# A three-stage kernel (attention, two MoE products): instructions freed from the written order from the last group of the first MoE on

## The chip, the cores and the metric

The kernel runs on one core of a Trainium2 chip. The metric is the device time of one execution in microseconds (us); less is better. A core has five engines that matter here: TensorE (PE, matmuls), VectorE (DVE), ScalarE (ACT), GpSimd (POOL) and SyncE (SP). SP computes nothing here: it issues the loads and stores, which 16 DMA engines carry out. Each engine takes the instructions of its own list in order, and an instruction that waits holds up those behind it.

## What is computed

The reference is an attention, then a product with a cosine gate, then a product with a rational gate. It comes down to:

```python
x = attention(rmsnorm(q) * g_q, rmsnorm(k) * g_k, v)   # 4 batches, 12 heads, 448 rows, 64 columns
x = x.transpose(0, 2, 1, 3).reshape(1792, 768)
h = x @ moe_w_in                                       # 768 x 2048
x = (h * cos(h)) @ moe_w_out                           # 2048 x 768
h = x @ moe2_w_in
P = a[0] + a[1] * h + a[2] * h**2 + a[3] * h**3
Q = 1.0 + abs(b[0]) * abs(h) + abs(b[1]) * h**2
out = (P / (Q + 1e-6)) @ moe2_w_out
```

## The kernel before

**Weights and numbers.** Every fp32 operand of a big product is kept as a high and a low half, and three matmuls take the place of one. A block of 128 columns of `w_in` is a tile "in f", a block of 128 rows of `w_out` a tile "out f", f from 0 to 15; either holds 768 KB with both halves. They are made once and stored in DRAM (`wd`), and loaded again with `load_w` whenever they are used. In this text "in f" and "out f" are tiles of the second MoE. They live in seven places (pool `w`), and from the second MoE on in nine (`w4` adds two).

**The first MoE** goes batch by batch, with the attention of the next batch in between. Its 16 blocks f are taken in four groups of four (`G`). In the last group of the last batch (`tail` in `run`) the six result tiles y are finished; each is split by ACT (high half) and by POOL or DVE (low half) into a tile x and stored to DRAM (`xd<-x`, the line with `self.xd[b, d]` in `moe1_second`).

**The second MoE** (`moe2`) makes two passes, over batches 0 and 1 and over batches 2 and 3. Its work comes in steps:

- A first product (`before`): 18 matmuls of in f with the x of one batch, into one of three PSUM places (`h3_ps`). Then comes the gate (`act2`): ACT makes q, v and w from the PSUM, DVE makes two products with it, which frees the PSUM, then ACT and DVE go on to the two halves of the tile g.
- A second product (`after`): 24 matmuls of four tiles out f with 128 rows of four tiles g, into one of two PSUM places (`o_ps`). ACT copies the first result of a row tile to o, DVE adds the other three to it, and after the fourth it is stored (`out<-o`). A pass has seven row tiles t.

First products of one group and second products of the group before alternate on PE. A group ends with its seventh second product; then the first product with the next group's first tile in f stands in the list. The four tiles out f of one group, the four tiles in f of the next and what is loaded ahead share the nine places: a tile's load overwrites a place whose old tile has been read for the last time.

**What sets the order.** Two things. First, `Clock`, a planner in the kernel: each step is given to it with a duration, and it hands the steps out in the order in which they would be ready. This order, in which the program's text is executed, is the written order. Second, the builder, which makes one list for each engine out of all instructions, with its own costs, and gives each tile one of its pool's places. It may reorder what doesn't depend on each other. The class `InOrder` stops it: each engine's handle (`self.nc.tensor` and so on, made in `Engines`) wraps every call and ties the new instruction to the last one of that engine (`add_manual_dep`, no semaphore). So before, every engine's list is the written order from the first instruction to the last. All instructions go through this helper, which is why the profile puts nearly all of them down to L193; tiles tell them apart.

Of the kernel before, what the change touches and what calls it, by code (L numbers as in the profile page):

```python
# [36 lines left out]
class Clock:  # L37
# [5 lines left out]
    def __init__(self):  # L43
        self.t, self.n, self.named = 0.0, 0, {}
        self.free = dict.fromkeys(("V", "A", "G", "S"), 0.0)
        self.todo = {e: [] for e in self.free}
        self.tab, self.dma = None, 0.0
# [133 lines left out]
class InOrder:  # L181


    def __init__(self, tc, engine):
        self.tc, self.engine, self.last = tc, engine, None

    def __getattr__(self, name):
        fn = getattr(self.engine, name)
        if not callable(fn):
            return fn  # L190

        def call(*args, **kw):
            inst = fn(*args, **kw)  # L193
            if hasattr(inst, "ins"):
                if self.last is not None:
                    info = mybir.DependencyInfo(
                        mybir.DependencyClass.NoSync, mybir.DependencyReason.DATA
                    )
                    self.tc.add_manual_dep(inst.ins, self.last.ins.name, info)
                self.last = inst  # L200
            return inst

        return call


class Engines:
# [4 lines left out]

    def __getattr__(self, name):
        return getattr(self.core, name)


class Kernel:
# [741 lines left out]
    def run(self):  # L958
        tc, nc, ck = self.tc, self.nc, self.ck
# [25 lines left out]
        def places(n, p, shape, dt, name):  # L985
            return Ring(n, lambda: p.tile(shape, dt, tag=name, name=name))
# [59 lines left out]
        def s_visits(ns):  # L1046

            it = s_chunks(ns)
            for k in ((1, 2, 3, 2, 2) if len(ns) == 2 else ()):
                fns = [next(it) for _ in range(k)]  # L1050
                yield lambda: [fn() for fn in fns]
            assert next(it, None) is None

        def v_visits(ns):

            a = [(n, kb) for n in ns for kb in range(NC)]
            for i in range(0, len(a) + 2, 2):
                yield lambda i=i: (
                    [self.att_va(st[n], kb) for n, kb in a[max(i - 2, 0) : i]],
                    [self.att_vt(st[n], kb) for n, kb in a[i : i + 2]],  # L1060
                )

        def take(it, k):
            for _ in range(k):
                fn = next(it, None)
                if fn is None:
                    return
                fn()
# [5 lines left out]
        def ring(name, n, shape, side="left"):  # L1074
            p = self.pool(name, n, side, PS)
            return p, Ring(n, lambda: p.tile(shape, F32, tag="t", name=name))
# [36 lines left out]
        def predecode(every):  # L1113
            steps[0] += 1
            flying[:] = [k for k in flying if k.end is None or k.end > ck.t]
            if ahead and steps[0] % every == 0 and len(flying) < 3:
                flying.append(self.decode(*ahead.popleft(), False, 4))

        m2 = None
        for b in range(B):  # L1120
            if b == B - 1:
                ck.emitted(*(("x", b, j) for j in range(NJ)), *chain.from_iterable(self.h_ring.used))
                self.close(x_ps, at_ps, self.at_p)
                self.close(h_ps)
                h_ps, self.h_ring = ring("h3_ps", 3, [P, 512])
                o_ps, self.o_ring = ring("o_ps", 2, [P, 2, 512], "right")
                nl2_p = self.pool("nl2", 1, "right")
                self.g2_ps, self.g2_n = [self.pool("g2", 5, "right")], 0
                yo_p = self.pool("yo", 2, "right")
                self.yo_ring = places(2, yo_p, [P, 2, S], F32R, "x")  # L1130
            vs = empty
            for g in range(NG):
                fs = list(range(g * G, g * G + G))
                gs = dict(head)
                head = {}
                if b == B - 1 and g == 1:
                    self.load_x(0, p=3)
                for f in fs:
                    if f not in gs:
                        gs[f] = self.moe1_first(b, f, lambda: take(vs, 1))  # L1140
                        if b:
                            predecode(2 if b < B - 1 else 1)
                for fn in vs:
                    fn()
                if g + 1 < NG:
                    head = {fs[-1] + 1: self.moe1_first(b, fs[-1] + 1)}
                elif b + 1 < B:
                    head = {0: self.moe1_first(b + 1, 0)}
                ss = vs = empty
                if b + 1 < B and g < 3:  # L1150
                    ns = [(b + 1) * NJ + 2 * g + i for i in range(2)]
                    ss = s_visits(ns)
                    vs = v_visits(ns)
                if g == 0:
                    if b:
                        ck.emitted(*(("xd", b - 1, d) for d in range(KD)))
                    y = self.y_p.tile([P, KD, S], F32, tag="y", name="y")
                tail = b == B - 1 and g == NG - 1
                if tail:
                    while ahead:  # L1160
                        self.decode(*ahead.popleft(), False, 4)
                    self.load_x(1)
                    self.nl_p, nl1_p = nl2_p, self.nl_p
                    m2 = self.moe2([0, 1], G, [2, 3])
                    lead, nxt = next(m2)
                for d in range(KD):
                    take(ss, 1)
                    self.moe1_second(b, d, fs, gs, y)
                    if b:
                        predecode(2 if b < B - 1 else 1)  # L1170
                    if tail and d % 2:
                        next(lead)
                for fn in ss:
                    fn()
                self.w_next(G)
# [47 lines left out]
```

## Time and profile before

| | us |
|---|---|
| median of three timed runs | 1334.45 |
| lowest, highest | 1333.38, 1335.68 |
| the profiled execution | 1326.99 |
| its span, first to last instruction | 1325.2 |
| PE busy in the span | 1251.3 |
| DVE busy | 918.8 |
| ACT busy | 671.0 |

The span is what the trace covers; 1.8 us of the profiled execution lie around it. The span has two parts here. Up to about 800 us come attention and the first MoE, of which the change leaves the order as it was; the second MoE follows up to the end at 1325.2. Times in the rows below count from the span's start.

### The profile page before, as it was taken

The numbers are of one execution on the slowest core, as the hardware profiler recorded it, in microseconds if no ns is written. First come the engines' busy times: TensorE is split into PE (matmuls) and PEld (weight loads), VectorE is DVE, ScalarE is ACT, GpSimd is POOL, SyncE is SP. The second block draws the span as 40 slices with busy tenths as digits, with TensorE's granted clock in tenths as the row PEclk, the third lists the DMA queues.
The fourth block names the chain that finished last, engine by engine and source line by source line (L and its number), as shares of the span: only waits on it lengthen the run. The fifth ranks groups of instructions, "written<-read, shape, count | busy, mean of one in ns | idle before, by whom it ended". The sixth has DMA issues, their size and how long they took to land.

```text
span 1325.2 us, 18179 instructions
## 1 busy us (share of the span) xinstructions
PE 1251.3 (94%) x6576; PEld 1066.0 (80%) x6576; DVE 918.8 (69%) x1422; ACT 671.0 (51%) x1277; POOL 326.0 (25%) x386
## 2 busy tenths in 40 slices
PE   5977999999999999999999998999999997989898
PEld 3545877678877868777789987998999887989898
DVE  6995889985967866886865465765676664556663
ACT  5764656553655645555533334754444443544440
POOL 5755336550434433444120221000000000000000
PEclk9888999999999999999999998999999998999999
DMA  4876786877878789878779997504043524141312
GB/s 121 247 242 229 248 278 222 257 259 285 274 254 288 230 290 330 299 230 319 264 275 390 368 353 296 181 1 190 25 167 101 232 79 195 34 181 41 150 48 84
DMA packets 133562, 283.63 MB, mean 214 GB/s; under 512 B 57952, under 2 KB 91744, under 8 KB 133472
## 3 DMA queue, kind: packets, MB, share of 16 engines
q1 hardware_dynamic: 133280, 282.46, 60.9%
q8 instruction: 52, 0.85, 0.3%
q14 instruction: 38, 0.31, 0.1%
q0 software_dynamic: 192, 0.00, 0.0%
HBM read 215.49 MB, written 66.93 MB: 213 GB/s over the span
## 4 chain that ended last, share of the span: by engine, by line
PE 79%; DVE 9%; DMA 6%; ACT 2%; SPq 2%; issue 1%; POOL 1%; DVEq 0%; ACTq 0%; POOLq 0%
PE h_ps L193 48%; PE o_ps L193 17%; PE at_ps L193 10%; PE x_ps L193 5%; DVE w L193 4%; DMA w<-wd 3%; DMA raw<-in_moe_w_in 2%; DVE mx L193 2%; SPq L193 2%; DVE k L193 1%; DMA x<-xd 1%; DMA ab<-in_moe_a 0%; ACT k L193 0%; POOL qk L193 0%; DVE sums L193 0%
## 5 line engine op out<-in xcount | busy, mean ns | idle before, releaser
L193 PE MATMUL h_ps<-x,w 128*128 128x448 f32 x2304 | 513.1, 377 | 35.5 <-DMA w<-wd 20.7
L193 PEld LDWEIGHTS h_ps<-x,w 128*128 128x128 f32 x2304 | 438.9, 193 | 87.6 <-issue 23.7
L193 PE MATMUL h_ps<-g,w 128*128 128x448 f32 x1152 | 251.6, 373 | 7.0 <-DVE k L193 5.2
L193 PEld LDWEIGHTS h_ps<-g,w 128*128 128x128 f32 x1152 | 217.9, 191 | 32.2 <-DVE k L193 6.6
L193 PE MATMUL o_ps<-w,g 128*128 128x384 f32 x1344 | 243.8, 337 | 0.0
L193 PEld LDWEIGHTS o_ps<-w,g 128*128 128x128 f32 x1344 | 236.8, 188 | 1.8
L193 DVE SCALAR_TENSOR_TENSOR w<-raw,w 128x768 int32<-128x768 int32 x128 | 146.9, 1150 | 0.7
L193 ACT ACTIVATE e<-at_ps,mx 128x448 f32<-128x448 f32 x168 | 104.9, 634 | 36.2 <-DVE mx L193 36.0
L193 POOL TENSOR_TENSOR raw<-w,raw 128x768 fp32r<-128x768 f32 x40 | 77.4, 1938 | 111.7 <-ACT raw L193 102.2
L193 PEld LDWEIGHTS at_ps<-ident,e 128*128 128x128 f32 (+1 forms) x696 | 77.1, 139 | 28.8 <-issue 21.2
L193 DVE TENSOR_REDUCE mx<-at_ps 128x1 f32<-128x448 f32 x168 | 94.9, 615 | 5.4 <-PE at_ps L193 4.9
L193 PE MATMUL x_ps<-et,v 128*64 128x448 f32 (+1 forms) x384 | 90.6, 568 | 8.0 <-DVE rb L193 5.2
L193 PE MATMUL at_ps<-kt,qt 64*128 64x448 f32 (+1 forms) x504 | 88.0, 412 | 5.1 <-DVE kt L193 2.6
L193 PE MATMUL at_ps<-ident,e 128*128 128x128 f32 (+1 forms) x696 | 89.9, 279 | 3.1 <-ACT e L193 3.1
L193 DVE TENSOR_TENSOR q<-q,h_ps 128x448 f32<-128x448 f32 x64 | 39.7, 621 | 68.2 <-ACT v L193 47.6
L193 ACT ACTIVATE k<-h_ps,cc 128x448 int32<-128x448 f32 x64 | 40.6, 634 | 86.4 <-PE h_ps L193 86.2
L193 PEld LDWEIGHTS at_ps<-kt,qt 64*128 64x128 f32 (+1 forms) x504 | 52.1, 195 | 37.8 <-issue 15.6
L193 ACT ACTIVATE g<-q 128x448 fp32r<-128x448 f32 x64 | 37.0, 578 | 86.0 <-DVE q L193 86.0
L193 ACT ACTIVATE r<-v,cc 128x448 f32<-128x448 f32 x64 | 42.9, 670 | 70.3 <-DVE v L193 70.2
L193 ACT ACTIVATE q<-h_ps,na 128x448 f32<-128x448 f32 x64 | 46.2, 722 | 52.9 <-PE h_ps L193 52.7
L193 DVE SCALAR_TENSOR_TENSOR q<-q,na,h_ps 128x448 f32<-128x448 f32 x64 | 43.5, 680 | 38.9 <-ACT w L193 38.9
L193 DVE SCALAR_TENSOR_TENSOR k<-k,h_ps 128x448 f32<-128x448 int32 x64 | 39.6, 618 | 44.5 <-ACT k L193 44.4
(75 smaller groups left out, 1392.3 us busy)
## 6 DMA issues: line engine op xcount, KB each, us to landing
w<-wd SPq DMA_DIRECT2D x168, 768.0 KB
wd<-raw SPq DMA_DIRECT2D x40, 768.0 KB
raw<-in_moe_w_in SPq DMA_DIRECT2D x32, 768.0 KB
raw<-in_moe_w_out SPq DMA_DIRECT2D x32, 768.0 KB
wd<-w SPq DMA_DIRECT2D x24, 768.0 KB
xd<-x SPq DMA_DIRECT2D x24, 448.0 KB
x<-xd SPq DMA_DIRECT2D x24, 448.0 KB
rb<-rd SPq DMA_DIRECT2D x48, 112.0 KB
```

Of the source, the lines that this page charges most:

```text
L193: inst = fn(*args, **kw)
```

## The change

`InOrder` gets a flag, `tied`. While it is true, each instruction is tied to its predecessor as before. `Engines.untie` sets it false for all five engines, and `run` calls that once, where the last group of the first MoE's last batch begins. From there on the builder may order each engine's list as it likes, as far as data and places allow. No instruction is added or taken away, no tile changes its size or its pool.

```diff
     def __init__(self, tc, engine):
-        self.tc, self.engine, self.last = tc, engine, None
+        self.tc, self.engine, self.last, self.tied = tc, engine, None, True
...
             if hasattr(inst, "ins"):
-                if self.last is not None:
+                if self.last is not None and self.tied:
                     info = mybir.DependencyInfo(
...
+
+    def untie(self):
+        for e in (self.tensor, self.vector, self.scalar, self.gpsimd, self.sync):
+            e.tied = False
...
                 tail = b == B - 1 and g == NG - 1
                 if tail:
+                    nc.untie()
                     while ahead:
                         self.decode(*ahead.popleft(), False, 4)
```

What the builder makes of it can be read in the built lists. PE's is the same but for three places, two of which are told of below; at the third, the first two result tiles of the first MoE's last group are interleaved. SP's, ACT's and DVE's lists differ at many places.

**SP, second pass, about the load of in 4.** Here w_10049 is out 1, w_10050 out 2, w_10354 out 3, w_10419 in 4, and out_0<-o are stores of results of the first pass. Before:

```order
L193 DMA w_10049<-wd_60 128x1536
L193 DMA w_10050<-wd_60 128x1536
L193 DMA out_0<-o_8590 128x768
L193 DMA out_0<-o_8656 128x768
L193 DMA out_0<-o_8726 128x768
L193 DMA out_0<-o_8792 128x768
L193 DMA w_10354<-wd_60 128x1536
L193 DMA out_0<-o_8857 128x768
L193 DMA w_10419<-wd_60 128x1536
```

The same stretch with the change:

```order
L193 DMA out_0<-o_8590 128x768
L193 DMA out_0<-o_8656 128x768
L193 DMA out_0<-o_8726 128x768
L193 DMA out_0<-o_8792 128x768
L193 DMA w_10050<-wd_60 128x1536
L193 DMA out_0<-o_8857 128x768
L193 DMA w_10354<-wd_60 128x1536
L193 DMA out_0<-o_8921 128x768
L193 DMA w_10419<-wd_60 128x1536
L193 DMA w_10049<-wd_60 128x1536
```

Out 1 moved from the head of the stretch to behind in 4, and the stores moved ahead of all the loads. In the built program the place of in 4 is the same in both lists, that of in 2, and the load waits for PE's last matmul with in 2.

**SP, second pass, about the load of in 8.** Here w_10552 and w_10553 are out 5 and out 6, w_10658 is out 7, w_10789 in 8 and w_10918 in 9. Rows with a minus are before, with a plus the change.

```order
-L193 DMA w_10552<-wd_60 128x1536
-L193 DMA w_10553<-wd_60 128x1536
 L193 DMA w_10658<-wd_60 128x1536
 L193 DMA w_10789<-wd_60 128x1536
 L193 DMA w_10918<-wd_60 128x1536
+L193 DMA w_10552<-wd_60 128x1536
+L193 DMA w_10553<-wd_60 128x1536
 L193 DMA w_11047<-wd_60 128x1536
```

Out 5 and out 6 moved behind in 9. Two tiles go the same way about in 12, one group later: out 10 and out 11 moved behind in 12, in 13 and in 14. In the first pass out 6, out 7 and in 8 keep their order, and so do out 11 and in 12; ahead of the second pass three of the six loads of batch 2's x moved ahead of in 0.

**PE, first pass, about the first product with in 8.** `h_ps<-x,w` is a first product, `o_ps<-w,g` a second one; g_8555, g_8692, g_8827 and g_8956 are the tiles g of f = 4 to 7.

```order
-L193 MATMUL h_ps<-x,w 128x448 x36
+L193 MATMUL h_ps<-x,w 128x448 x18
 L193 MATMUL o_ps<-w,g_8555 128x384 x6
 L193 MATMUL o_ps<-w,g_8692 128x384 x6
-L193 MATMUL o_ps<-w,g_8827 128x384 x6
+L193 MATMUL o_ps<-w,g_8827 128x384 x2
+L193 MATMUL h_ps<-x,w 128x448 x18
+L193 MATMUL o_ps<-w,g_8827 128x384 x4
 L193 MATMUL o_ps<-w,g_8956 128x384 x6
```

The 18 matmuls with in 8 moved behind 14 matmuls of the second product that used to follow them. At the start of the second pass a like thing is done: the first product with in 0 is split in 12, 3 and 3 matmuls, with 3 and 4 matmuls of a second product in between.

On ACT the four later copies that make the high halves of the first MoE's result (`x<-y`, the tiles x_8213, x_8232, x_8289 and x_8310) moved back: x_8213 from behind the first gate of the second MoE into the second gate, x_8232 to where x_8289 stood, x_8289 and x_8310 into the third gate. On SP the load of in 3 moved from behind the fifth of the six stores of that result to ahead of it.

## Rows read from the trace of the kernel before

**Rows 1.** Waits of PE, 815 us to the end: us in total, times, longest.

```profile
PE h_ps L193 <- DMA w<-wd: 20.7, 4, 9.2
PE h_ps L193 <- DVE v L193: 4.0, 1, 4.0
PE h_ps L193 <- DMA x<-xd: 3.1, 3, 2.6
```

**Rows 2.** Timeline of PE: start, length in us, instruction, count [idle before <- releaser].

```profile
823.40 24.35 PE L193 MATMUL h_ps<-x,w 128*128 128x448 f32 x108 [4.65 <-DMA w<-wd]
...
906.06 5.47 PE L193 MATMUL h_ps<-x,w 128*128 128x448 f32 x18 [2.71 <-DMA w<-wd]
...
967.37 3.88 PE L193 MATMUL h_ps<-x,w 128*128 128x448 f32 x18 [0.63 <-DVE g L193]
...
1029.48 4.18 PE L193 MATMUL h_ps<-x,w 128*128 128x448 f32 x12 [2.63 <-DMA x<-xd]
...
1035.05 0.88 PE L193 MATMUL h_ps<-x,w 128*128 128x448 f32 x3 [0.26 <-DMA x<-xd]
...
1079.39 3.88 PE L193 MATMUL h_ps<-x,w 128*128 128x448 f32 x18
1083.10 4.34 PE L193 MATMUL o_ps<-w,g 128*128 128x384 f32 x24
...
1100.36 5.65 PE L193 MATMUL h_ps<-x,w 128*128 128x448 f32 x18 [9.21 <-DMA w<-wd]
...
1165.84 5.39 PE L193 MATMUL h_ps<-x,w 128*128 128x448 f32 x18 [4.16 <-DMA w<-wd]
...
1230.40 5.47 PE L193 MATMUL h_ps<-x,w 128*128 128x448 f32 x18 [3.97 <-DVE v L193]
```

**Rows 3.** Busy us (count) of PE, PEld, DVE, ACT, POOL; granted clock, DMA share, GB/s.

```profile
1100.00:1106.00 6.00, 5.64 (x19) 5.14 (x20) 0.00 (x0) 0.00 (x0) 0.00 (x0) 0.65 1.02 421
```

**Rows 4.** Timeline of SP, its issues of loads and stores: start, length, what, count.

```profile
896.48 2.44 SPq L193 DMA_DIRECT2D w<-wd  x3
...
1019.98 1.38 SPq L193 DMA_DIRECT2D w<-wd  x2
1021.41 4.56 SPq L193 DMA_DIRECT2D x<-xd  x6
...
1084.35 0.80 SPq L193 DMA_DIRECT2D w<-wd  x2
1085.24 2.06 SPq L193 DMA_DIRECT2D out<-o  x4
1087.35 0.49 SPq L193 DMA_DIRECT2D w<-wd  x1
1087.93 0.53 SPq L193 DMA_DIRECT2D out<-o  x1
1088.71 0.40 SPq L193 DMA_DIRECT2D w<-wd  x1
...
1155.87 2.10 SPq L193 DMA_DIRECT2D w<-wd  x4
...
1220.67 1.83 SPq L193 DMA_DIRECT2D w<-wd  x3
```

**Rows 5.** Waits of the SP queue, 837 us to the end.

```profile
SPq L193 <- PE o_ps L193: 249.9, 16, 56.4
```

**Rows 6.** Timelines of SP and POOL about the load of in 3.

```profile
808.83 9.70 SPq L193 DMA_DIRECT2D xd<-x  x3
818.62 18.45 SPq L193 DMA_DIRECT2D w<-wd  x6
...
817.02 1.15 POOL L193 TENSOR_TENSOR x<-y,x 128x448 fp32r<-128x448 f32 x1 [6.73 <-ACT x L193]
```

**Rows 7.** Timelines of ACT and DVE: a gate's first ACT step, its second DVE step.

```profile
836.95 0.71 ACT L193 ACTIVATE q<-h_ps,na 128x448 f32<-128x448 f32 x1
...
839.45 0.68 DVE L193 SCALAR_TENSOR_TENSOR q<-q,na,h_ps 128x448 f32<-128x448 f32 x1 [0.70 <-ACT w L193]
```

## The prediction

> **What bounds the kernel now.** I first asked the trace who TensorE (PE) waited for from 815 us to the end. [rows 1] is the answer that matters: 20.7 us in four waits for a weight tile's load, 4.0 us for one that the trace puts down to VectorE (DVE), 3.1 us for three loads of the activations x. Then I read PE's timeline over the second MoE [rows 2]. Its normal steps are a first product of 18 matmuls in 3.88 us (3.71 us from its start at 1079.39 to the next start at 1083.10, since the ends overlap by 0.17) and a second product of 24 matmuls in 4.34 us, or 4.17 without the overlap, 0.18 us each. Between those PE runs without a gap except at seven places, which I call a to g in the order of time. The bracket is the idle time; the row's length shows a second loss, for most of the groups that follow a wait take about 5.5 us where 3.88 us is normal. [rows 3] shows why: from 1100 to 1106 us the granted clock is 0.65 of full speed, so the chip gave PE part of that stretch at 1.2 GHz instead of 2.4 after it had stood idle.
>
> Next I read the queue on SyncE (SP), which issues every load and store [rows 4]. An instruction there waits in its place in the list, and all behind it wait too. [rows 5] says for what: 249.9 us of the queue's waiting was for a second product (o_ps) to finish, in 16 waits, the longest 56.4 us. That is a load of "out" weights, waiting for the last reader of the tile place that it will overwrite, with the "in" weights that PE needs first listed behind it.
>
> **The change, part by part.** It adds no arithmetic. What it moves is worth what becomes of the seven waits, so I price each as its idle time plus the slow group behind it.
>
> e, before in 4 of the second pass: 9.21 idle plus 5.65 - 3.88 = 1.77, so 10.98 us [rows 2]. The load of in 4 was issued at 1088.71, behind out 1 and out 2 (1084.35), four stores, out 3 and a fifth store [rows 4]; it needed only that the first product in 2 of batch 3 be over, which it was at 1079.39 + 3.88 = 1083.3 [rows 2]. Now the stores stand first and no longer wait behind out 1, out 2 and out 3 go as their own places come free, and in 4 stands ahead of out 1. It can be issued at 1083.3. The price of a load with little before it: that of in 3 was issued at 818.62 [rows 6] and PE started on it at 823.40 [rows 2], 4.78 us. So it is there at 1088.1, and PE asks for it at 1091.2. Out 1, now behind it, is issued at about 1084.4 and lands some 1.9 us after it (0.786 MB at the 421 GB/s of [rows 3]), near 1090; it is asked for near 1096. Gain 11.0 us, nothing late next.
>
> f, before in 8: 4.16 + 5.39 - 3.88 = 5.67 us. In 8 was the last of four loads issued from 1155.87 on [rows 4], behind out 5 to out 7; out 5 and out 6 waited for the last second product of the group. Now out 7, in 8 and in 9 stand ahead of both. In the built program they wait for first products of in 4 to in 6; the last of these ends two pairs of groups, 2 x (3.71 + 4.17) = 15.8 us, before the need, the one for in 8 four pairs, 31 us. Out 5 and out 6 are then two loads issued near 1155, there by 1155.87 + 4.78 + 1.9 = 1162.6, asked for after 1166. Gain 5.7 us.
>
> g, before in 12: 3.97 + 5.47 - 3.88 = 5.56 us. The trace names DVE as releaser, but the built program makes this group wait only for in 12 and for a DVE step on the third first product before it, long done. In 12 was the third load of the run from 1220.67 on [rows 4]. Three loads in a row, 4.78 + 2 x 1.9 us, end near 1229.2, and PE starts at 1230.40. So I take it as a load, moved exactly as in f. Gain 5.6 us; bounds 0 (if it is DVE) and 5.6.
>
> b, before in 8 of the first pass: 2.71 + 5.47 - 3.88 = 4.30 us. Here out 6, out 7 and in 8 keep their order and their issue from 896.48 on [rows 4], so in 8 lands when it did. What changes is PE's list: 14 matmuls of the next second product now stand ahead of in 8's first product, and their weights (out 4 to out 6) are there or are the first of that run. 14 x 0.18 = 2.5 us of the 2.71 is filled, and an idle time of about 0.2 us should not slow the clock: c shows 0.63 us idle and then 3.88 us [rows 2]. Gain 4.0 us; bounds 0 and 4.3.
>
> d, before the x of the second pass: idle 2.63 in front and 0.5 us in two short pieces inside, and 4.18 + 2 x 0.88 - 3.88 = 2.06 for slow matmuls, 5.2 us. [rows 2] has the first and the last of its three pieces; the middle one, of three matmuls too, has no row here and is taken to be like the last. In 0 and in 1 went at 1019.98, then six x loads from 1021.41 [rows 4]. Now three of the x loads stand ahead of in 0 and go when PE has read the x that they replace: in 0 waits for the sixth matmul of a second product, and that reading stands in the first product just ahead of it, so near 1019.98 - 1.1 - 3.7 + 0.6 = 1015.8. In 0 keeps its time. Only the other three come behind in 1, three tiles earlier than before; at 0.459 MB and 421 GB/s, 1.1 us each, the last lands some 3 us sooner, near 1031.6 instead of 1035.05. PE's list lets 3 + 4 second-product matmuls in between the last x groups. I leave 0.7 us. Gain 4.5 us; bounds 2 and 5.2.
>
> c: out 11 and in 12 keep their order. Gain 0.
>
> a, before in 3: 4.65 us idle, then a run of six groups in 24.35 us where 6 x 3.71 is 22.3, so up to 6.7 us. The load now stands ahead of the fifth store of the first MoE's result, but still behind the fourth. In the old run the queue was held at the fifth until 818.5, because its low half was made by GpSimd from 817.02 on [rows 6]. On ScalarE (ACT) each of these copies has moved one step back, and the fourth now stands where the fifth stood. So the load goes out at about the same time. Gain 0; bounds -0.5 (ACT and DVE steps now wait in another order) and +6.7.
>
> Sum: 11.0 + 5.7 + 5.6 + 4.0 + 4.5 = 30.8 us. Against the profiled execution, 1326.99, that is 1296.2. The three timed runs have a median of 1334.45, 7.5 us more than that execution; I take the same gain off it: **1303.6 us**. A measurement of this kernel tells about 0.2% (2.7 us) from no change.
>
> One rule of the Trainium skill speaks against most of this. The page "Perfetto Trace Analysis", section "Optimization Strategy", says that the same gap repeating on the saturated engine can mean that memory for the next tile is short. By that rule the gaps at b, e, f and g would stay whatever the order, and only d would gain, 4.5 us. The trace disagrees for e, where the place was free 5.4 us before the issue; for b it agrees.
>
> **The rivals.** *The places are late, not the queue.* The tile places are nine for the weights; if the loads at f and g can't go earlier because the place of in 8 or in 12 itself comes free late, those two waits stay and the gain is 30.8 - 11.3 = 19.5 us: 1315 us. For it: waits repeat once per group of four. This is what is left of the page's rule once e is taken out by its rows. Against: the waits in the built lists, 31 us ahead of the need, as worked out under f. 14%.
>
> *The first wait goes too.* If ACT gets to the fourth copy 3 us sooner than I reckon, because DVE no longer runs beside GpSimd there, a shrinks to 1 us or so and the clock stays up: 36 us gained, 1298 us or a little less. 8%.
>
> *Slower: the activation chain blocks the PSUM ring.* The free order puts the next group's first ACT step (which waits for PE) ahead of finishing steps of the group before. The three PSUM places for first products come back when DVE has done its second step. Now that takes from 836.95 to 840.13, 3.2 us [rows 7], and PE returns to the same place after two more groups, at least 2 x 3.71 = 7.4 us. It decides once 4.2 us are added. At 1 us lost for each of the 64 first products, 1334.45 - 30.8 + 64 = 1368 us; slower than before from 0.5 us each on. Against: over the second MoE ACT and DVE are idle a good part of each group. 4%.
>
> *No effect.* The order that the builder finds could be the written one wherever it counts, or the timed runs could be held by something else than these waits: 1334 us. Against: the lists differ at five of the seven waits. 4%.
>
> **How the numbers follow.** The forecast, all of b, d, e, f, g near their terms, has 70%. The range 1296 to 1314 takes in the second rival, the bounds of a, b and d, those of g and the nearer part of the place rival; it leaves out the rest of that one and the two last. Faster by over 0.2%: 70 + 14 + 8 = 92, plus half of the "no effect" case that still gains a little, 93%; within 0.2%: 3%; slower: 4%.
>
> **What would show it.** Right: PE's waits for weight tiles from 815 us on fall from 20.7 to about 6 us, nearly all at a and c; the groups after in 4, in 8 and in 12 of the second pass take 3.88 us; the longest waits of the SP queue are for h_ps or DVE's o, with in 4, in 8 and in 12 issued over 5 us before their use; PE's busy sum falls by some 8 us as slow matmuls go. Wrong: PE waits of several us put down to DVE or ACT that recur in each group; a wait at f or g as long as now; a wait at a over 6 us.

## The result, and the profile after

The changed kernel took 1297.45 us in the median of four runs (1296.18 to 1302.72), the kernel before 1333.91 us beside it: a ratio of 0.9738, with a 95% interval of 0.9703 to 0.9772. In a later series, again beside the kernel before, it was 1299.06 us and 0.9767 (0.9751 to 0.9783). The forecast was 1303.6 us with a range of 1296 to 1314. The profiled execution is the one of 1296.18 us, with a span of 1294.2 us; PE is busy for 1239.1 us of it (1251.3 before).

The waits of PE from 795 us to the end, in the kernel after (us in total, times, longest). They answer to [rows 1]:

```profile
PE h_ps L193 <- DMA w<-wd: 5.2, 3, 4.5
PE h_ps L193 <- ACT g L193: 0.6, 1, 0.6
```

Of 20.7 us for weight tiles 5.2 are left, and the waits for x and for DVE are gone. The timeline of PE shows the places one by one (start, length, instruction, count, [idle before <- releaser]); it answers to [rows 2]:

```profile
780.92 11.11 PE L193 MATMUL h_ps<-x,w 128*128 128x448 f32 x54
...
794.41 2.51 PE L193 MATMUL h_ps<-g,w 128*128 128x448 f32 x11 [0.97 <-DVE g L193]
797.53 1.74 PE L193 MATMUL h_ps<-g,w 128*128 128x448 f32 x6 [0.61 <-ACT g L193]
799.11 3.81 PE L193 MATMUL h_ps<-x,w 128*128 128x448 f32 x18
...
824.42 24.42 PE L193 MATMUL h_ps<-x,w 128*128 128x448 f32 x108 [4.48 <-DMA w<-wd]
...
904.35 2.61 PE L193 MATMUL o_ps<-w,g 128*128 128x384 f32 x14
907.40 3.88 PE L193 MATMUL h_ps<-x,w 128*128 128x448 f32 x18 [0.45 <-DMA w<-wd]
...
964.39 3.89 PE L193 MATMUL h_ps<-x,w 128*128 128x448 f32 x18 [0.32 <-DMA w<-wd]
...
1020.07 6.36 PE L193 MATMUL h_ps<-x,w 128*128 128x448 f32 x30
1026.27 0.68 PE L193 MATMUL o_ps<-w,g 128*128 128x384 f32 x3
...
1071.11 3.88 PE L193 MATMUL h_ps<-x,w 128*128 128x448 f32 x18
...
1078.99 7.59 PE L193 MATMUL h_ps<-x,w 128*128 128x448 f32 x36
...
1138.39 7.59 PE L193 MATMUL h_ps<-x,w 128*128 128x448 f32 x36
...
1197.31 7.59 PE L193 MATMUL h_ps<-x,w 128*128 128x448 f32 x36
```

Wait a (824.42) is as it was. At b, 14 matmuls of a second product stand in front of in 8, as the change put them, and 0.45 us of idle is left. At d the six groups of x follow with no idle at all. At e, f and g (the three rows of 36 matmuls) two first products run as one row: there is no gap ahead of in 4, in 8 and in 12. So a place is priced best from the start of one group to the start of the next group that both kernels have:

| stretch, ended by | before | after | change | predicted |
|---|---|---|---|---|
| run of 54 to first product of in 0 | 19.68 | 18.19 | -1.49 | not seen |
| to the second product behind a | 49.68 | 49.57 | -0.11 | 0 |
| to the next first product behind b | 67.95 | 64.20 | -3.75 | -4.0 |
| to the second product behind c | 55.54 | 55.24 | -0.30 | 0 |
| to the first product behind d | 68.87 | 63.55 | -5.32 | -4.5 |
| to the second product behind e | 65.89 | 54.75 | -11.14 | -11.0 |
| to the second product behind f | 65.23 | 59.40 | -5.83 | -5.7 |
| to the second product behind g | 64.64 | 58.92 | -5.72 | -5.6 |
| to the end of the span | 89.49 | 89.46 | -0.03 | 0 |

The sum is -33.69 us. The first line is a stretch that the prediction did not read, for it began at 815 us. In the timeline of PE before, ahead of [rows 2]:

```profile
778.23 11.11 PE L193 MATMUL h_ps<-x,w 128*128 128x448 f32 x54
...
792.75 0.47 PE L193 MATMUL h_ps<-g,w 128*128 128x448 f32 x1 [1.59 <-ACT g L193]
793.41 4.67 PE L193 MATMUL h_ps<-g,w 128*128 128x448 f32 x14 [0.18 <-DVE g L193]
```

Here 14 matmuls took 4.67 us, which at the rate of a row of 24 in 5.03 us take 2.9. That is the slow clock and not the written order: from 793.4 to 798 us the granted clock is 0.63 of full speed, so PE was at 1.2 GHz for most of it. A kernel told of below, before_10, has the lists of the kernel before, and its PE stands for the same two waits there, but the 14 matmuls take 3.12 us, at a granted clock of 1.00:

```profile
797.71 0.47 PE L193 MATMUL h_ps<-g,w 128*128 128x448 f32 x1 [1.59 <-ACT g L193]
798.37 3.12 PE L193 MATMUL h_ps<-g,w 128*128 128x448 f32 x14 [0.18 <-DVE g L193]
```

Its first line of the table is 18.13 us, no longer than the 18.19 after. So the 1.49 us are scatter of one execution, and what the edit brings is nearer 32.2 us than 33.7. The run of 54 is the last row that the edit can't touch. It began 2.69 us later in the run after (780.92 for 778.23), and -33.69 + 2.69 is the -31.0 us between the two spans.

On SP the waiting has changed sides. Waits of the SP queue, 837 us to the end, after (they answer to [rows 5]), and its timeline at the loads of in 4, in 8 and in 12 and at wait a ([rows 4, 6]):

```profile
SPq L193 <- PE h_ps L193: 272.0, 33, 15.5
SPq L193 <- PE o_ps L193: 73.9, 22, 26.6
```

```profile
815.68 3.91 SPq L193 DMA_DIRECT2D xd<-x  x2
819.68 0.38 SPq L193 DMA_DIRECT2D w<-wd  x1
...
1075.01 2.41 SPq L193 DMA_DIRECT2D w<-wd  x3
...
1110.48 0.32 SPq L193 DMA_DIRECT2D w<-wd  x1
...
1169.67 0.32 SPq L193 DMA_DIRECT2D w<-wd  x1
```

The row of 1075.01 begins with in 4. It goes out when PE's last product with in 2, whose place it takes, ends: at 1071.11 + 3.88 = 1074.99. PE takes it up as the second half of its row of 1078.99, at 1078.99 + 3.71 = 1082.7, 7.7 us on. In 8 and in 12 go out 31.6 and 31.4 us before their use (1142.1 and 1201.0); the prediction had 31. The load of in 3 (819.68) still stands behind the fourth store, the second of the two in the row of 815.68.

### The profile page after: what moved, and what is told of

It is laid out like the page before. It is cut to its first block, busy times and chain, and to the rows that moved or that the text cites. A ratio compares the mean times of both kernels' runs of the same rounds, so it can differ in the third digit from the quotient of the medians.

```text
span 1294.2 us, 18192 instructions
## 1 busy us (share of the span) xinstructions
PE 1239.1 (96%) x6576; PEld 1055.6 (82%) x6576; DVE 918.4 (71%) x1422; ACT 667.6 (52%) x1277; POOL 324.4 (25%) x386
## 4 chain that ended last, share of the span: by engine, by line
PE 82%; DVE 9%; DMA 3%; POOL 1%; issue 1%; SPq 1%; ACT 1%; DVEq 0%; ACTq 0%; POOLq 0%
PE h_ps L193 50%; PE o_ps L193 18%; PE at_ps L193 10%; DVE w L193 5%; PE x_ps L193 4%; DVE mx L193 2%; DMA w<-wd 1%; DMA raw<-in_moe_w_in 1%; SPq L193 1%; DVE k L193 1%; POOL qk L193 1%; POOL w L193 0%; DMA ab<-in_moe_a 0%; DVE sums L193 0%; DVE qt L193 0%
## 5 line engine op out<-in xcount | busy, mean ns | idle before, releaser
L193 PE MATMUL h_ps<-x,w 128*128 128x448 f32 x2304 | 504.5, 372 | 12.3 <-DMA w<-wd 5.2
L193 PEld LDWEIGHTS h_ps<-x,w 128*128 128x128 f32 x2304 | 433.2, 190 | 61.2 <-issue 9.8
L193 PEld LDWEIGHTS h_ps<-g,w 128*128 128x128 f32 x1152 | 215.1, 189 | 33.1 <-DVE k L193 7.6
L193 DVE SCALAR_TENSOR_TENSOR v<-v,r 128x448 f32<-128x448 f32 x64 | 40.5, 633 | 40.3 <-ACT r L193 37.8
L193 DVE SCALAR_TENSOR_TENSOR q<-q,na,h_ps 128x448 f32<-128x448 f32 x64 | 43.5, 680 | 31.4 <-ACT w L193 31.4
```

## Experiments

Every engine of a kernel here is either tied to the written order or free from the same point on as in the change. "From the 54" is the time from the start of that run of 54 matmuls to the end of the span in the profiled execution: it leaves out what no edit touches, and is 546.97 us before and 513.28 after. Medians are of four runs (pe_only one, adp ten), ratios to the kernel before in the same series with 95% intervals. Since 546.97 has the slow clock ahead of in 0 in it, each gain is up to 1.5 us too large.

| kernel | free | median | ratio | from the 54 | gain |
|---|---|---|---|---|---|
| changed | all five | 1297.45 | 0.9738 (0.9703 to 0.9772) | 513.28 | 33.7 |
| sp_only | SP | 1304.17 | 0.9776 (0.9739 to 0.9814) | 518.53 | 28.4 |
| pe_only | PE | 1303.91 | one run | 516.87 | 30.1 |
| not_sp | all but SP | 1310.54 | 0.9837 (0.9809 to 0.9866) | 524.14 | 22.8 |
| adp | ACT, DVE, POOL | 1337.29 | 1.0045 (1.0017 to 1.0074) | 553.81 | -6.8 |
| sp_pe | SP, PE | 1292.14 | 0.9700 (0.9673 to 0.9727) | 506.79 | 40.2 |
| not_act | all but ACT | 1299.82 | 0.9760 (0.9732 to 0.9788) | 513.52 | 33.5 |
| before_10 | none, ten places | 1309.77 | 0.9831 (0.9803 to 0.9858) | 524.40 | 22.6 |
| sp_pe_store_pool | SP, PE | 1294.72 | 0.9719 (0.9690 to 0.9749) | 509.00 | 38.0 |
| after_again | all five | 1299.06 | 0.9767 (0.9751 to 0.9783) | 513.48 | 33.5 |
| sp_pe_again | SP, PE | 1292.14 | 0.9713 (0.9694 to 0.9733) | 508.11 | 38.9 |
| sp_pe_10 | SP, PE, ten places | 1294.35 | 0.9729 (0.9714 to 0.9743) | 508.72 | 38.3 |
| sp_pe_all | SP, PE, from the first instruction | 1295.94 | 0.9748 (0.9730 to 0.9765) | 506.05 | 40.9 |

**Which list carries the gain?** First SP's alone, then all but SP's, PE's alone, and both:

```diff
     def untie(self):
-        for e in (self.tensor, self.vector, self.scalar, self.gpsimd, self.sync):
-            e.tied = False
+        self.sync.tied = False
```

> Only the queue on SP is untied; PE, DVE, ACT and POOL keep the written order. Theory 1 (the order of SP's list carries e, f, g and part of d; PE's list carries b): e, f and g gone, b as before (about 2.7 us idle and a slow group, 4.3 us in all), c and a unchanged, 0.7 to 2.5 us left at d. Gain 25 to 27 us: a profiled time near 1301. Rival (the tile places are late, or the free order of ACT and DVE is what brings the loads forward): e, f, g stay mostly as before and the time is above 1315.

Theory 1 held for e, f and g: they are gone with PE's list as it was before, and so is most of d (0.78 us left). The gain is 28.4 us for the 25 to 27 expected; the profiled execution took 1307.09 us and not 1301, since its 54 began 8.3 us later than in the kernel before. At a and b PE's timeline says:

```profile
837.64 3.91 PE L193 MATMUL h_ps<-x,w 128*128 128x448 f32 x18 [0.29 <-DVE q L193]
845.26 10.28 PE L193 MATMUL h_ps<-x,w 128*128 128x448 f32 x36 [3.71 <-DVE q L193]
...
913.83 3.95 PE L193 MATMUL h_ps<-x,w 128*128 128x448 f32 x18 [2.69 <-DMA w<-wd]
```

b stays with 2.69 us, but without the slow group. And a is not what was expected: the load of in 3 is in time (there is no wait for it), and in its place PE waits 3.71 us for DVE's q and then runs 36 matmuls in 10.28 us, for which 7.6 is normal. PE's list has seven first products in a row there and three PSUM places, and DVE is next in line behind the load.

```diff
-        for e in (self.tensor, self.vector, self.scalar, self.gpsimd, self.sync):
+        for e in (self.tensor, self.vector, self.scalar, self.gpsimd):
```

> All engines but SP are untied, so the list of loads and stores is the written one. Theory 1: only b is filled, and c to g stay with their old idle times (e 9.2, f 4.2, g 4.0, d 2.6 and less): a gain of about 4 us, profiled near 1322. Rival (ACT's and DVE's order, which frees places and halves earlier, carries the gain): e, f, g shrink to under 2 us each, time near 1300.

```diff
     def untie(self):
-        for e in (self.tensor, self.vector, self.scalar, self.gpsimd, self.sync):
-            e.tied = False
+        self.tensor.tied = False
```

> Only PE is untied. Theory 1: as with all engines but SP untied, about 4 us gained at b and nothing elsewhere, 1322 to 1323. Rival (the filled matmuls need ACT's and DVE's free order to be there in time): PE waits for g of the second product at b instead, no gain, 1327.

Both theories fell, and in the same way. SP's list is the written one, and still e, f and g are nearly gone (one wait of 1.02 us for a weight tile is left at them in not_sp). That is what the rival of not_sp foretold, but not by ACT's and DVE's order, for in pe_only those are the written ones. PE's timeline of not_sp at a, and of pe_only at e, f and g:

```profile
834.93 24.82 PE L193 MATMUL h_ps<-x,w 128*128 128x448 f32 x108 [13.13 <-DMA w<-wd]
```

```profile
1095.04 2.35 PE L193 MATMUL o_ps<-w,g 128*128 128x384 f32 x12 [1.07 <-DMA w<-wd]
1097.73 11.21 PE L193 MATMUL h_ps<-x,w 128*128 128x448 f32 x54 [0.35 <-DMA w<-wd]
...
1154.00 3.88 PE L193 MATMUL h_ps<-x,w 128*128 128x448 f32 x18 [0.43 <-DMA w<-wd]
...
1212.31 3.92 PE L193 MATMUL h_ps<-x,w 128*128 128x448 f32 x18 [0.47 <-DMA w<-wd]
```

The builder does not keep PE's list when SP's is tied: it makes another one, in which second products of the new group stand ahead of the first product whose tile comes late (the rows of o_ps ahead of the first products with in 4). The loads are as late as before (in 4 goes out 1.5 us after the start of the last first product ahead of it in pe_only, 1085.23 - 1083.74, and 1.4 before, 1088.71 - 1087.28), and PE has other work. So "either list will do": SP's brings the load forward, PE's fills the wait. The theory that only b lies with PE's list was true of the changed kernel's list, not of what a free PE list can do. And a is 13.13 us in not_sp, for 4.65 before: with SP's list as written, something in the free ACT and DVE lists makes in 3's load later. The next kernel has that alone.

```diff
-        for e in (self.tensor, self.vector, self.scalar, self.gpsimd, self.sync):
+        for e in (self.vector, self.scalar, self.gpsimd):
```

> ACT, DVE and POOL untied; SP and PE keep the written order. Theory 1 (SP's or PE's list is what brings the gain, either will do): b to g stay with their old idle times (b 2.7, c 0.6, d 3.1, e 9.2, f 4.2, g 4.0), and a grows, since ACT's free order makes the fourth and fifth copy later while in 3's load still stands behind the fifth store: a near 13 us, as in the kernel with all but SP untied. So slower than before by 6 to 9 us: 1333 to 1336 profiled against 1327. Rival (the free order of ACT and DVE brings part of the gain at e, f, g): those shrink by 2 us or more each and the time is under 1325.

This is the control: SP's and PE's lists are those of before. PE's timeline:

```profile
832.23 23.83 PE L193 MATMUL h_ps<-x,w 128*128 128x448 f32 x108 [9.23 <-DMA w<-wd]
...
1108.44 5.71 PE L193 MATMUL h_ps<-x,w 128*128 128x448 f32 x18 [9.38 <-DMA w<-wd]
...
1174.42 5.22 PE L193 MATMUL h_ps<-x,w 128*128 128x448 f32 x18 [4.60 <-DMA w<-wd]
...
1239.02 5.31 PE L193 MATMUL h_ps<-x,w 128*128 128x448 f32 x18 [4.18 <-DMA w<-wd]
```

e, f and g stay, slow groups and all, and a doubles: theory 1 held, with 9.23 us at a for the 13 expected and 1335.39 us for the profiled execution. The median is 0.45% longer than before (0.17 to 0.74%). The last row also tells what g is: the same place with nearly the same idle time, and here the trace names the weight load where [rows 1] named DVE. That g goes with SP's list alone (sp_only) says the same.

```diff
-        for e in (self.tensor, self.vector, self.scalar, self.gpsimd, self.sync):
+        for e in (self.tensor, self.sync):
```

> SP and PE untied, ACT, DVE and POOL in the written order. Theory 1: the whole gain but for a us at most, 1295 to 1298 profiled; b, c, d, e, f, g as in the changed kernel. Rival (ACT, DVE and POOL matter): over 1300, with waits of PE for g or o of the ACT or DVE side that the changed kernel does not have.

Better than theory 1 had it: 5 to 7 us faster than the changed kernel, so ACT's, DVE's and POOL's free order does not help, it costs. PE's timeline tells where. From the 54 to the first product of in 0 it is 16.11 us for 18.19 in the changed kernel; from there until eleven first and two second products are done, which takes in a, 60.02 for 65.47.

**What keeps wait a?** ACT's timeline has the copies that the stores wait for (`x<-y`). The fourth starts 10.15 us after the first product of in 0 in the kernel before (808.06 and 797.91) and 18.34 us after it in the changed one (817.45 and 799.11). The two rows, first before, then after:

```profile
808.06 0.58 ACT L193 ACTIVATE x<-y 128x448 fp32r<-128x448 f32 x1 [0.62 <-DMA xd<-x]
```

```profile
817.45 0.56 ACT L193 ACTIVATE x<-y 128x448 fp32r<-128x448 f32 x1
```

So ACT alone was tied:

```diff
-        for e in (self.tensor, self.vector, self.scalar, self.gpsimd, self.sync):
+        for e in (self.tensor, self.vector, self.gpsimd, self.sync):
```

> All engines but ACT untied. Theory 1: what keeps wait a at 4.5 us in the changed kernel is ACT's free order, which makes the fourth copy of the first MoE's result late and with it the store ahead of in 3's load. With ACT tied the load goes out near 816 to 817 and a falls to 1 us or less, with the matmuls behind it at full clock: 1290 to 1293, as with SP and PE alone untied. Rival (DVE's order, or PE's, makes the difference there): a stays above 3 us and the time is 1296 to 1298.

Half right. PE's timeline shows the load's wait gone: the load of in 3 goes out at 815.76, 15.4 us after the first product of in 0 (20.6 in the changed kernel). But the time, 1299.82 us, is no better, for the wait has moved to DVE, as in sp_only; that is the rival's first half. SP's and then PE's timeline:

```profile
811.60 2.97 SPq L193 DMA_DIRECT2D xd<-x  x2
815.76 0.32 SPq L193 DMA_DIRECT2D w<-wd  x1
```

```profile
829.72 3.91 PE L193 MATMUL h_ps<-x,w 128*128 128x448 f32 x18 [1.22 <-DVE q L193]
837.33 6.31 PE L193 MATMUL h_ps<-x,w 128*128 128x448 f32 x18 [3.70 <-DVE q L193]
```

With SP and PE alone free the same place reads, in PE's timeline of sp_pe:

```profile
833.88 3.91 PE L193 MATMUL h_ps<-x,w 128*128 128x448 f32 x18 [0.78 <-DVE q L193]
837.63 3.52 PE L193 MATMUL o_ps<-w,g 128*128 128x384 f32 x19
841.51 7.57 PE L193 MATMUL h_ps<-x,w 128*128 128x448 f32 x36 [0.36 <-DVE q L193]
```

The two kernels have the same lists on SP, ACT and POOL, and on PE the same up to the fifth of these first products (the row of 833.88, in not_act that of 837.33). What differs is DVE's list: free, it makes the fourth and the fifth wait 4.92 us; as written, 0.78. The sixth waits 0.36 us in sp_pe, behind 19 matmuls of a second product that PE's free list put there, and 3.71 us in sp_only, where nothing stands there. The stretch about a named above is 66.75 us in not_act, 66.26 in sp_only, 66.42 in pe_only and 60.02 in sp_pe, for 65.51 before: anything is gained at a only with the load early (SP), PE's list free and DVE's as written, all three. ACT's free order delays the load; what that would cost at a with DVE's list as written, no run shows. It does cost 2.1 us ahead of in 0, where not_act has 16.09 us and the changed kernel 18.19.

```diff
+            eng = nc.gpsimd if b == B - 1 else nc.sync
             def store():
-                nc.sync.dma_start(
+                eng.dma_start(
```

With this, and SP and PE alone free:

> SP and PE alone untied, and the six stores of the last batch's first-MoE result are issued by GpSimd's queue instead of SP's, so that no load stands behind them. Theory 1: with SP and PE alone untied the load of in 3 is hardly late any more (PE waits for DVE there, 0.8 and 0.4 us), so little is left: 0 to 1.5 us better than that kernel, 1290 to 1294. Rival (GpSimd's own work or its queue is held by the issue of the stores, and the low halves come later): 2 us or more slower than that kernel.

The load of in 3 goes out 31.5 us after the start of the 54 (814.10 - 782.60), and in sp_pe, behind four stores, 31.5 us after it as well (816.71 - 785.21). So where the copies keep their written order the stores are not what holds it. The median is 2.6 us above that of sp_pe, with waits of PE of 0.92 us for the load and 1.93 for DVE's q about a. That is on the rival's side, but the intervals overlap, so the runs leave open whether it is slower.

**Order or places?** One more place for weight tiles, everything else as before, in the written order:

```diff
-        self.w_ps = [self.pool("w4", 2)] * 2 + [w_p] * 7
+        self.w_ps = [self.pool("w4", 3)] * 3 + [w_p] * 7
```

> The kernel before, all in the written order, with one more place for weight tiles in the second MoE (ten for nine). Theory 1 (the written order of the queue is what makes the loads late, not the number of places): the queue on SP still waits for tiles in the wrong order, e stays over 6 us, and the gain is under 10 us: 1318 to 1327 profiled. Rival (the Trainium skill's page Perfetto Trace Analysis, section Optimization Strategy: a gap that repeats means that memory for the next tile is short): e, f and g all go to under 1 us, over 20 us gained, 1305 or less.

Theory 1 fell: 22.6 us gained with the lists of all engines unchanged. The rival is not met in full either (2.21 us left at e, 1309.40 us for its 1305). PE's timeline:

```profile
826.17 24.54 PE L193 MATMUL h_ps<-x,w 128*128 128x448 f32 x108 [4.00 <-DVE q L193]
...
1030.97 6.42 PE L193 MATMUL h_ps<-x,w 128*128 128x448 f32 x18 [5.95 <-DMA x<-xd]
...
1094.81 3.89 PE L193 MATMUL h_ps<-x,w 128*128 128x448 f32 x18 [2.21 <-DMA w<-wd]
...
1154.71 3.90 PE L193 MATMUL h_ps<-x,w 128*128 128x448 f32 x18 [0.34 <-DMA w<-wd]
```

At e 2.21 us are left of 9.21, at f 0.34 of 4.16, at g 0.54 of 3.97, and at b 0.21 of 2.71; d is longer than before (5.95), and a is now DVE's. In [rows 5] the queue waits for second products because the load at its head needs a place; with a tenth place it waits 172.6 us for them in place of 249.9. So the Trainium skill's page "Perfetto Trace Analysis", section "Optimization Strategy", names a cause whose remedy works here, though it is not the only one. With both lists free and ten places:

> SP and PE alone untied, and ten places for weight tiles for nine. Theory: order and places buy the same waits, so with both free lists the tenth place has 1 to 2 us left to take (the waits under 0.9 us): 1289 to 1292. Rival (places and order add up): more than 5 us below the kernel with nine places.

Nothing is added: 1294.35 us beside 1292.14 for nine places in the same series, ratios that overlap. Not even the 1 to 2 us expected came. Order and places buy the same waits.

**The best version and the spread.** The changed kernel and sp_pe, on the same chip:

> The changed kernel once more, beside the kernel with SP and PE alone untied on the same chip, to pin what the free order of ACT, DVE and POOL is worth. From the start of the 54 matmuls ahead of the first MoE's last second products to the end of the span the profile had 513.3 us, against 547.0 before: the theory expects the same here within 1 us, wherever that start lies in the run, and a median of 1296 to 1299.

> SP and PE alone untied, once more. The profile had 506.8 us from the start of those 54 matmuls to the end, 6.5 us less than the changed kernel. If the free order of ACT and DVE costs those 6.5 us (the late fourth copy at wait a, and no matmuls moved ahead of it), the median is 1290 to 1293 and the ratio to the changed kernel on the same chip is near 0.995. If the earlier difference came from the part of the run that neither kernel touches, the two are within 0.2%.

Both hold, but for a first median 0.06 us above its range: 513.48 and 508.11 us from the 54, medians of 1299.06 and 1292.14, 6.9 us or 0.53% apart, and the two ratios to before do not overlap. The version with SP and PE alone free beats both kernels. Last, SP and PE free from the first instruction on:

```diff
         for e in ("tensor", "vector", "scalar", "gpsimd", "sync"):
             setattr(self, e, InOrder(tc, getattr(tc.nc, e)))
+        self.untie()
```

> SP and PE untied from the first instruction, so also in attention and the first MoE, where PE still waits for some 50 us in all. If what held for the second MoE holds there (PE's list filled with work that is ready, loads in the order in which their places come free), 5 to 25 us are gained over untying them late: 1267 to 1287. Rival (in the first part the waits are for DVE and ACT, whose lists stay as written, and the builder's costs for them are wrong, so PE is given steps whose data come late): slower than 1300.

Neither: 1295.94 us, where sp_pe_again in the same series has 1292.14. The 54 start at 785.25 us there, inside the 778.2 to 786.6 of the kernels whose first part is as written. So the runs show no gain in that part; its longest waits of PE are for DVE (18.6 us for qk, 8.5 us for k), whose list is the written one.

## Why the prediction was right, and where it was not

**e, f, g** (11.0, 5.7, 5.6; measured 11.14, 5.83, 5.72). Right in size and cause. In 4 goes out as its place comes free and not 5.4 us later. sp_only moves SP's list alone and they go; adp leaves SP's and PE's and they stay. That PE's free list or a tenth place would remove them as well, the prediction did not see.

**b** (4.0; measured 3.75) and **d** (4.5; measured 5.32). At b the filling is PE's list, for in sp_only 2.69 us stay. But the price of the wait held the slow group of the one profile: in sp_only the same wait costs 2.8 us and not 4.3. At d the 0.7 us that were to be left are not there.

**c** gave 0.30, and the stretch ahead of in 0 1.49 us, which is the clock in the execution of before and not the edit. All the same "from 815 us to the end" was too late a start: the edit does reach that stretch. In the changed kernel two things cancel there. PE's free list makes it 16.1 us (sp_pe, not_act) for 18.1 as written (before_10), and ACT's free order makes it 18.2 again.

**a** (0; measured 0.11). The two opposite moves that the prediction set against each other are both there and large: the load ahead of the fifth store, and the fourth copy 8.2 us later on ACT. Its upper bound of 6.7 us was too high for an earlier load alone: sp_only and not_act have that, and DVE then stops PE for 3.7 us in the same run of first products. That it would be DVE was not foreseen. The second rival, with wait a gone, is reached only with ACT, DVE and POOL tied. That the changed kernel's median lies at its 1298 us all the same is chance: wait a stayed.

**The rule of the Trainium skill's page "Perfetto Trace Analysis".** The prediction said that by it the gaps would stay whatever the order, and that the trace disagrees for e, since the place of in 4 was free 5.4 us before the issue. The gaps did go with nine places. But to set the queue against the places, as the first rival does, was too sharp: the loads listed ahead of in 4 were waiting for places, and a tenth one took most of e away as well.

**The base.** The gain was taken off the median of the timed runs, 7.5 us above the profiled execution; 1297.45 is 6.2 us under the 1303.6 so worked out. Of that 0.5 us are the base (1333.91 was measured beside it for 1334.45) and 5.7 the gain, 36.5 us between these two medians for 30.8. In the later series the gain between the medians is 31.2 us, and between the two profiles 33.7, or 32.2 without the slow clock ahead of in 0. So most of the miss is scatter and not a term of the sum. The part that no edit touches shows how large it is: in thirteen profiled executions in which it is the same program, the 54 start between 778.23 and 786.57 us, median 782.76, and that of before is the earliest of all. So its profile was some 4.5 us short beside a common one, and the one of after 1.8.

**The signs named.** PE's waits for weight tiles fell to 5.2 us, for about 6 foretold, and the groups after in 4, in 8 and in 12 run at the normal 3.88 us. PE's busy sum fell by 12.2 us, for some 8. The sum of SP's waits moved to h_ps as said, but the longest single one is still for o_ps, 26.6 us.

## What to carry to other kernels

Where an engine that issues loads waits in its list, ask what the loads behind it would need, and price each wait of the busy engine from group start to group start. A late load had three cures here that do much the same work: its queue's order (28.4 us), other work for the engine that waits (30.1 us, one run) and one more place (22.6 us). Their gains do not add: the first two together gave 39 to 40 us, and the third on top nothing. And undoing one alone need not bring the wait back where a scheduler is free to use another (not_sp). Free only the lists that gain by it: here ACT's, DVE's and POOL's free order cost 5 to 7 us of what SP's and PE's bring.

## What was not expected of the hardware

The same idle time did not always bring the slow clock. One case is the pair of rows ahead of in 0 shown above, before and before_10: the same waits of 1.59 and 0.18 us, then a granted clock of 0.63 in the one (793.4 to 798 us) and 1.00 in the other (798.4 to 801.4), with the same load on the DMA engines (shares of 1.01 and 1.02). Another: ahead of in 8 in the first pass PE stood 2.71 us in the kernel before and 2.69 in sp_only, after the same work. Busy us (count) of PE, PEld, DVE, ACT, POOL; granted clock, DMA share, GB/s; first before, then sp_only:

```profile
898.00:903.00 5.00, 5.00 (x28) 4.67 (x26) 3.08 (x5) 2.46 (x4) 0.00 (x0) 1.00 0.94 348
...
906.00:911.60 5.60, 5.54 (x20) 5.03 (x21) 3.02 (x5) 1.37 (x3) 0.00 (x0) 0.70 1.01 421
```

```profile
906.00:911.00 5.00, 5.00 (x27) 4.46 (x25) 2.88 (x5) 2.62 (x4) 0.00 (x0) 1.00 0.88 321
...
913.80:918.00 4.20, 4.17 (x21) 3.87 (x22) 2.72 (x5) 1.52 (x3) 0.00 (x0) 1.00 0.60 247
```

Behind the wait the clock was 0.70 of full speed in the one, PE being at 1.2 GHz for part of it, and 1.00, 2.4 GHz throughout, in the other; the wait cost 4.3 us and 2.8. The Trainium skill's page "TensorE: Matmul & The Clock Gate", Part 1, says that the number of slow matmuls at a kernel's start differs between runs of one kernel. These rows are from the middle of a run and show the like there; they show no cause. A term for the clock behind a wait of this length is therefore a bound, not a price.
